# A fused attention and two-layer kernel: state rows times w_in in plain float32, one batch at a time

## The chip, the cores and the metric

The kernel runs on one core of one Trainium2 chip. The metric is the device time of one execution in microseconds (us); less is better. The shapes are fixed, and the program is fully unrolled: every instruction stands in one of the engines' instruction streams, in an order fixed when the program is built.

## What is computed

```python
scores = 0.125 * x @ state.T          # per batch b (8) and head h (8); x 512x64, state 32x64
a = softmax(scores); xread = a @ state
a2 = softmax(0.125 * state @ x.T); sread = a2 @ x
x = concat([xread, sread], rows)      # 544 rows per batch, 8 heads side by side: 4352 x 512
h = x @ w_in;  g = s * relu(h)**2 + b;  x = g @ w_out        # 512 -> 2048 -> 512
h = x @ w_in2; g = h * sigmoid(h);      out = g @ w_out2     # 512 -> 2048 -> 512
```

## The kernel before, in words

All the weights come in as 64-bit numbers and are made into 32-bit ones on the chip. `load64` fetches a pair of weight units (a unit is 128x512 numbers, 512 KB raw) into one of two `raw` buffers, `absw` (L189, ScalarE, "A" below) takes the absolute value of the high words, and `bits` (four VectorE steps at L197, L201, L206 and L211, "B") shifts and joins the words. The first layer has 16 units of w_in (i0 to i15) and 16 of w_out (o0 to o15).

A matmul here runs on TensorE in the rounded 32-bit type `float32r`, in one pass. To keep the accuracy, an operand is split into a rounded part and a rest (`hi_w` on ScalarE, `lo_w` on VectorE by way of `rest`, L232), and each product takes three matmuls: high times high, high times low, low times high. A matmul on operands of type plain float32 needs no split.

The first layer's input x is `a @ state` for the 512 rows of a batch, so the kernel doesn't form it. It forms G = state @ w_in for each batch and head (32 rows per head), and then `a @ G` for the batch: `mm1_a` (L566, "M1") multiplies G with the transposed softmax weights `at_h`, `at_l`. G is made once for all batches, at the start: `produce(u, p, at)` (L275) takes the unit u of w_in and the pair p of batches, and does three `float32r` matmuls 128x128x512 (L281) with the split state `sgh`, `sgl`. There are 16 units and 4 pairs, so 192 matmuls. Its result is copied out of PSUM (L229): for pairs 1 to 3 whole (`xr`, 128x512), for pair 0 in halves of 64 rows, one per batch (`pull_g`). `keep_g` writes it to `gd` in DRAM; `load_g` later fetches what a batch needs, and `split_g` splits it. Batch 0 is taken straight on (`first_g`).

The program has these stages on TensorE: the first block (batch 0: G for all batches, the softmax of batches 0 and 1, the conversion and split of all 32 units, and batch 0 through the first layer), then seven blocks for batches 1 to 7 and one for the state rows ("s"), each 16 x (M1 of 6 matmuls, `mm2` of 12 matmuls, L628, "M2"), then the second layer (`first_product` and `Chunks`, L902).

The order of the first block is written out by hand in the table `FIRST`, which `first()` reads name by name: L load of a weight pair, A and B its conversion, H and O (with i or o) the split of a unit, Sh and Sl the split of the state, P a `produce`, E the copy out of PSUM, D the write to `gd`, F the split of batch 0's G, M1, R (relu), S (square), T (times s, plus b), U (split), M2, and names with p or q the steps of the softmax of a half (four heads) of a batch. A star puts a step on VectorE that otherwise runs on ScalarE. Each engine takes its steps in the order of the table. PSUM has eight banks of 128x512: four (`ps_o`) accumulate M2's result, two (`ps_h`) take M1's, two (`ps_a`) are for the rest. In the later blocks `run` sets the order, with M2 three steps behind M1, and `extra` hangs the loads, the splits and the next batch's softmax between them.

A tile has the name of its place in SBUF (`v3`, `wh5`, `xr1`); the trace leaves the numbers out. `bank` is a tile in PSUM.

Of the kernel before, what the change touches and what calls it, by code (L numbers as in the profile page):

```python
# [22 lines left out]
P = 128  # L23
# [23 lines left out]
A.4 Lsbd.1 B.3.1 B.3.2 E.3.2 R.0 D.3.2 B.4.0 E.4.1 P.5.3.o B.3.3 R.1 D.4.1 M1.2 S.0 E.4.3 B.4.1
B.4.2 M1.3 S.1 D.4.3 Ho.1* Lxn.0.0 T.0 L.5 P.4.2.o R.2 F.2.0 p1mm.a E.4.2 Eb.5 B.4.3 Hi.6* E.5.1
D.4.2 Oi.6 P.5.2.o U.0.0 D.5.1 P.6.0.a Hi.7* p1rd Ho.0* Oo.1 T.1 P.6.2.h S.2 P.6.3.o E.5.3 D.5.3
p1nb p0sr.o Eb.6 U.1.0 D.5.0 Oo.0 U.0.1 Oi.7 Ea.6 p1ex P.6.1.o p1tr L.6 p0pu A.5 U.1.1  # L50
P.7.0.a E.5.2* D.5.2 R.3 P.7.1.a E.6.1 T.2* B.5.0 P.7.3.h E.6.3 D.6.3 S.3 M2.0 D.6.0 Ea.7 D.6.1
T.3 U.2.0 B.5.1 B.5.2 B.5.3 L.7 p1n0 F.3.0 M2.1 Eb.7 U.3.0 F.2.1 Hi.8 F.3.1 A.6 Oi.8 U.2.1
E.6.2 P.8.0.a M1.4 B.6.0 E.7.3 D.7.3 E.7.1 p1mx B.6.1 D.6.2 D.7.1 D.7.0 Lxn.1.0 Eb.8 U.3.1 R.4
Ho.2 B.6.2 M1.5 M1.6 D.8.0 Oo.2 p1n1 Ea.8 R.5 S.5 P.7.2.a P.8.1.h p1n2* R.6 B.6.3 A.7 P.8.3.a
p1sb L.8 M2.2 B.7.0 B.7.1 Ho.3 Hi.9 E.8.3 D.8.3 E.7.2 Oi.9 D.7.2 B.7.2 Oo.3 S.4 P.9.1.h
P.9.0.a S.6 T.4 U.4.0* p1en p1tu.a B.7.3 M2.3 E.8.1 D.8.1 p1s0 Eb.9 Ea.9 p1pl U.4.1 Ho.4
Hi.10* A.8 L.9 D.9.0 Oo.4 P.8.2.a P.9.3.h Oi.10 T.6 p1sr.a B.8.0 E.8.2 p1s1 E.9.1 B.8.1 E.9.3
p1s2 p1pu D.9.3 F.4.0 D.9.1 B.8.2 B.8.3 D.8.2 Lxt.1.1 P.10.0.h T.5 Ea.10 U.5.0 F.4.1 p1s3 L.10
Ho.5 Hi.11 Oo.5 A.9 p1s4 P.10.3.a M1.7 Oi.11 Eb.10 P.10.1.a M2.4 R.7 B.9.0 B.9.1 P.11.0.h
U.5.1 U.6.0 E.10.3 P.9.2.h Ea.11 Eb.11 D.10.3 q1mm.a E.10.1 D.10.1 S.7 B.9.2 B.9.3 E.9.2  # L60
P.11.1.h M2.5 Lsbd.2 F.5.0 q1rd Hi.12 L.11 U.6.1 Lg.0.0 Ho.6 F.5.1 A.10 Oi.12 E.11.1
B.10.0 B.10.1 M1.8 M1.9 q1nb D.9.2 D.11.1 D.10.0 B.10.2 p1ah T.7 R.8 U.7.0 Lxn.1.1 P.12.1.a R.9
B.10.3 q1tr P.11.3.h q1ex P.10.2.h q1n0 Oo.6 P.12.0.a S.8 E.11.3 M2.6 Ho.7 Hi.13* Oi.13
D.11.0 L.12 A.11 Ea.12 U.7.1 E.12.1 T.8* Oo.7 E.10.2 D.10.2 M1.10 B.11.0 B.11.1 S.9
Gh.0.0 U.8.0 D.11.3 Eb.12 D.12.1 M1.11 T.9 q1n1 q1n2* B.11.2 M2.7 B.11.3 U.9.0 R.10 U.8.1 L.13
Hi.14 q1tu.a A.12 Ho.8* Oo.8 P.11.2.a q1pl q1mx P.13.0.h R.11 P.12.3.a B.12.0 E.11.2 D.11.2
q1sr.a U.9.1 B.12.1 S.10 E.12.3 Eb.13 D.13.0 P.13.1.a q1pu Ea.13 D.12.0 D.12.3 Oi.14
P.14.0.h B.12.2 B.12.3 Hi.15* P.13.3.a S.11 E.13.1 D.13.1 Ea.14 P.12.2.h Ho.9 M2.8 Gl.0.0
E.12.2 Oi.15 D.12.2 A.13 q1sb q1en L.14 Oo.9 B.13.0 Eb.14 P.14.1.a E.13.3 P.15.0.h E.14.1 F.6.0*
q1s0 P.13.2.h B.13.1 B.13.2 B.13.3 Ea.15 D.14.1 P.15.1.a Eb.15 D.15.0 q1s1 P.14.2.a  # L70
# [17 lines left out]
def fused_kernel(ctx: ExitStack, tc, xt, xn, sbd, sg, w1, w2, sv, bv, out):  # L88
# [22 lines left out]
    turn = [0]  # L111

    def bank(at, shape):

        if at == "o":
            at = f"o{turn[0] % NC}"
            turn[0] += 1
        pool = {"h": ps_h, "a": ps_a}.get(at, ps_o)
        return pool.tile(list(shape), F32, tag=at, name="bank")

    def space(tag, shape=(P, S), dtype=F32R):
        return wpool.tile(list(shape), dtype, tag=tag, name=tag)

# [7 lines left out]
    xr = [space(f"xr{c}", dtype=F32) for c in range(NC)]  # L131
# [11 lines left out]
    again = [False]  # L143

    def tags(w):
        t, i = w
        if t == "o":
            return f"wh{i}", f"wl{i}"
        i = AGAIN[i] if again[0] else NU - RING + i % RING
        return f"v{2 * i}", f"v{2 * i + 1}"  # L150

    def load64(pair):
        t = rot("raw", 2, (P, 2, S, 2), U32)
        raw[pair] = t.rearrange("p i n t -> p (i n) t")
        for i, (k, u) in enumerate(pair):
            src = w1 if k in "io" else w2
            nc.sync.dma_start(
                out=t[:, i],
                in_=src[u + NU * (k in "oO")].bitcast(U32).rearrange("p (n t) -> p n t", t=2),
            )  # L160

    def new32(pair):
        t = rot("wf", 2, (P, 2 * S))
        w32[pair] = t
        for i, w in enumerate(pair):
            w32[w] = t[:, i * S:(i + 1) * S]

    def load32(pair):
        for t, u in pair:
            w32[t, u] = space(f"mid{u % 4}", dtype=F32)  # L170

            fg, c = divmod(u, NC)
            for q in range(4):
                r = q % 2 * D + c % 2 * NS
                nc.sync.dma_start(
                    out=w32[t, u][q * NS:(q + 1) * NS],
                    in_=kept[t, NC * fg + c // 2 * 2 + q // 2][r:r + NS],
                )
# [4 lines left out]
    def absw(pair, i=None):  # L183
        if not i:
            new32(pair)
        hi, tf = raw[pair][:, :, 1], w32[pair]
# [4 lines left out]
    def bits(pair, op, i=None):  # L191
        lo, hi, tf = raw[pair][:, :, 0], raw[pair][:, :, 1], w32[pair]
# [23 lines left out]
    def reorder(pair, i):  # L216

        x = w32[pair[i]]
        w32[pair[i]] = to = space(f"v{24 + i}", dtype=F32)
# [13 lines left out]

    def hi_w(w, dve=False):
        wh[w] = space(tags(w)[0])
        copy(wh[w], w32[w], dve)

    def lo_w(w):
        wl[w] = space(tags(w)[1])
        rest(wl[w], w32[w], wh[w])  # L240

    def split(hi, lo, x):
# [7 lines left out]
    sg_t, sgh, sgl = {}, {}, {}  # L250
    gd = {
        (p, fg): dram.tile([NC * P, S], F32, name=f"gd{p}_{fg}")
        for p in range(B // 2) for fg in range(4)
    }
    G = {}

    def load_sg(p):
        sg_t[p] = space(f"v{12 + p}", dtype=F32)
        nc.sync.dma_start(out=sg_t[p], in_=sg[p])

    def hi_sg(p, dve):
        sgh[p] = space(f"wh{12 + p}")
        copy(sgh[p], sg_t[p], dve)

    def lo_sg(p):
        sgl[p] = space(f"wl{12 + p}")
        rest(sgl[p], sg_t[p], sgh[p])

    def new_g(b, fg):
        i = 4 * ((4 * b + fg) % 3)  # L270
        G[b, fg] = [[space(f"v{i + 2 * j + k}") for k in range(2)] for j in range(2)]

    gp = {}
# [1281 lines left out]
```

## Time and profile before

| | |
|---|---|
| median of 3 runs | 1329.31 us (1329.28 to 1331.46) |
| span of the profiled execution, first to last instruction | 1328.2 us |
| the profiled execution's own time | only its span is given; it lies 1.1 us under the median of the runs |
| TensorE matmul busy | 1304.2 us (98%), 6928 instructions |
| VectorE busy | 993.5 us (75%) |
| ScalarE busy | 739.7 us (56%) |
| mean granted TensorE clock | 0.999 of full |

The trace holds one execution, with the start and the length of every instruction. An engine's busy time is a union over its instructions. Matmuls overlap: the next starts while the results of the one before still drain, so their cost is the distance between starts, not the recorded length. On VectorE, too, an instruction that doesn't depend on the one before starts a little before that one's record ends. "Idle before" is the time in which an engine had nothing running, and the releaser is what it waited for.

### The profile page before, as it was taken

What the parts mean: (1) busy time and instruction counts of PE and PEld (TensorE: products, weight loads), DVE (VectorE), ACT (ScalarE), POOL (GpSimd) and SP (SyncE); (2) the same over time, 40 slices, a digit from 0 to 9 for tenths busy, and PEclk for the clock granted to TensorE, in tenths of its full rate; (3) what the DMA queues carried; (4) which work ended last, traced back from release to release, by engine and by line L of the source; (5) the groups of instructions that cost most, each with busy time, mean ns of one, the idle gap of its engine ahead of it and who ended that gap; (6) DMA issues with size and microseconds to landing.
All of it is one profiled execution on the core that took longest, in us unless ns stands there. A gap on an engine that the chain in (4) does not pass through costs nothing.

```text
span 1328.2 us, 20865 instructions
## 1 busy us (share of the span) xinstructions
PE 1304.2 (98%) x6928; PEld 1131.3 (85%) x6928; DVE 993.5 (75%) x1794; ACT 739.7 (56%) x1360; POOL 0.7 (0%) x7
## 2 busy tenths in 40 slices
PE   5999999999999999999999999999999999999997
PEld 3678787878787878888988888999998888999997
DVE  8999797979797979865966757576777765565654
ACT  7999564555454545544665646465666634353541
POOL 0000000000000000000000000000000000000000
PEclk9999999999999999999999999999999999999999
DMA  8988556464655545434568475657699796777583
GB/s 305 306 302 281 208 191 198 157 223 143 212 174 201 177 158 167 161 107 134 179 198 293 175 259 190 240 181 242 222 320 357 264 278 186 198 221 230 170 258 86
DMA packets 182925, 284.01 MB, mean 214 GB/s; under 512 B 25632, under 2 KB 99360, under 8 KB 182816
## 3 DMA queue, kind: packets, MB, share of 16 engines
q1 hardware_dynamic: 182016, 282.28, 64.4%
q8 instruction: 54, 0.88, 0.3%
q10 hardware_dynamic: 800, 0.39, 0.1%
q14 instruction: 55, 0.45, 0.1%
HBM read 166.72 MB, written 115.87 MB: 213 GB/s over the span
## 4 chain that ended last, share of the span: by engine, by line
PE 92%; ACT 2%; DMA 2%; DVE 2%; issue 1%; SPq 0%; ACTq 0%
PE bank L902 49%; PE o L628 27%; PE ph L566 14%; DMA raw<-w 2%; PE bank L281 1%; ACT xr L229 1%; ACT wf L189 0%; PE bank L390 0%; PE bank L377 0%; DMA gd<-xr 0%; PE bank L503 0%; DVE wf L211 0%; DVE v L232 0%; DVE wf L197 0%; DVE wl L232 0%
## 5 line engine op out<-in xcount | busy, mean ns | idle before, releaser
L566 PE MATMUL ph<-xh,v 128*128 128x512 f32 (+1 forms) x640 | 205.2, 372 | 0.1
L628 PE MATMUL o<-gh,wh 128*128 128x512 f32 (+1 forms) x448 | 169.5, 378 | 0.0
L628 PE MATMUL o<-gh,wl 128*128 128x512 f32 (+1 forms) x448 | 169.3, 378 | 0.0
L628 PE MATMUL o<-gl,wh 128*128 128x512 f32 (+1 forms) x448 | 169.3, 378 | 0.0
L566 PEld LDWEIGHTS ph<-xh,v 128*128 128x128 f32 x640 | 117.2, 188 | 26.5 <-issue 5.0
L608 DVE SCALAR_TENSOR_TENSOR r<-r,s_sb 128x512 f32<-128x512 f32 (+1 forms) x128 | 91.4, 714 | 42.6 <-ACT r L607 42.3
L566 PE MATMUL ph<-xl,v 128*128 128x512 f32 (+1 forms) x320 | 117.8, 368 | 0.0
L607 ACT ACTIVATE r<-ph 128x512 f32<-128x512 f32 (+1 forms) x128 | 71.8, 561 | 81.6 <-PE ph L566 79.1
L613 ACT ACTIVATE gh<-r,b_sb 128x512 fp32r<-128x512 f32 (+1 forms) x96 | 66.5, 693 | 56.2 <-DVE r L608 55.9
L628 PEld LDWEIGHTS o<-gh,wl 128*128 128x128 f32 x448 | 84.3, 188 | 15.8
L628 PEld LDWEIGHTS o<-gl,wh 128*128 128x128 f32 x448 | 84.3, 188 | 15.5
L628 PEld LDWEIGHTS o<-gh,wh 128*128 128x128 f32 x448 | 84.3, 188 | 15.5
L902 PE MATMUL bank<-v,v 128*128 128x384 f32 (+1 forms) x304 | 91.6, 360 | 0.0
L902 PE MATMUL bank<-wh,v 128*128 128x384 f32 (+1 forms) x254 | 83.0, 355 | 0.0
L614 DVE SCALAR_TENSOR_TENSOR gl<-r,b_sb,gh 128x512 fp32r<-128x512 f32 (+1 forms) x96 | 68.5, 714 | 15.4 <-ACT gh L613 15.3
L628 PE MATMUL o<-v,wh 128*128 128x512 f32 (+1 forms) x256 | 75.1, 377 | 0.0
L566 PEld LDWEIGHTS ph<-xl,v 128*128 128x128 f32 x320 | 60.4, 189 | 9.5
L902 PE MATMUL bank<-wl,v 128*128 128x384 f32 (+1 forms) x183 | 61.4, 356 | 0.0
L902 PEld LDWEIGHTS bank<-v,v 128*128 128x128 f32 x304 | 56.4, 188 | 5.7
L628 PEld LDWEIGHTS o<-v,wh 128*128 128x128 f32 x256 | 46.9, 188 | 9.1 <-DVE o L641 0.5
L211 DVE SCALAR_TENSOR_TENSOR wf<-raw,wf 128x512 uint32<-128x512 uint32 (+1 forms) x65 | 52.9, 814 | 2.0
L206 DVE SCALAR_TENSOR_TENSOR wf<-raw,wf 128x512 uint32<-128x512 uint32 (+1 forms) x65 | 52.3, 804 | 0.2
(1059 smaller groups left out, 3163.2 us busy)
## 6 DMA issues: line engine op xcount, KB each, us to landing
raw<-w SPq DMA_DIRECT2D x80, 512.0 KB, 4.9
gd<-xr SPq DMA_DIRECT2D x48, 256.0 KB, 3.4
v<-gd SPq DMA_DIRECT2D x192, 64.0 KB, 2.2
go<-v SPq DMA_DIRECT2D x58, 192.0 KB, 2.2
go<-v SPq DMA_DIRECT2D x38, 256.0 KB, 2.3
v<-go SPq DMA_DIRECT2D x34, 256.0 KB, 4.4
v<-go SPq DMA_DIRECT2D x41, 192.0 KB, 3.6
wh<-go SPq DMA_DIRECT2D x39, 192.0 KB, 3.5
```

Of the source, the lines that this page charges most:

```text
L206: nc.vector.scalar_tensor_tensor(out=t, in0=lo, scalar=29, in1=t, op0=ALU.logical_shift_right, op1=ALU.bitwise_or,)
L211: nc.vector.scalar_tensor_tensor(out=t, in0=hi, scalar=0xC0000000, in1=t, op0=ALU.bitwise_and, op1=ALU.bitwise_or,)
L229: nc.scalar.activation(out=out, in_=x, func=AF.Copy)
L281: nc.tensor.matmul(t, a[p][:, cs], x[w], start=i == 0, stop=i == 2)
L566: nc.tensor.matmul(ph[:, :n], a, x, start=j == 0 and i == 0, stop=j == last and i == 2)
L607: nc.scalar.activation(out=r, in_=ph[:, :n], func=AF.Relu)
L608: nc.vector.scalar_tensor_tensor(out=r, in0=r, scalar=s_sb, in1=r, op0=ALU.mult, op1=ALU.mult)
L613: nc.scalar.activation(out=gh, in_=r, func=AF.Identity, bias=b_sb)
L614: nc.vector.scalar_tensor_tensor(out=gl, in0=r, scalar=b_sb, in1=gh.bitcast(F32), op0=ALU.add, op1=ALU.subtract)
L628: nc.tensor.matmul(po[c][:, :n], a, x, start=f == 0 and i == 0, stop=f == NF - 1 and i == 2)
L902: nc.tensor.matmul(bank[:, :n], a, x, start=start and j == 0 and i == 0, stop=stop and j == last and i == 2, skip_group_check=True,)
```

## The change

- **produce** works on one batch b and a group fg of four units, straight from the converted units `w32` and the unsplit state `sg_t`: eight matmuls in plain float32, each with 64 rows (one head) by 32 columns by 512, for four units and two heads each. They are laid so that the four units go to the four 32-row strips of the result, and the two heads to two banks: one tile 128x2x512 over two PSUM banks holds the whole G of this batch and group. There are 32 such steps (8 batches by 4 groups).
- The splits of w_in's 16 units and of the state (Hi, Oi, Sh, Sl) are gone from the first block.
- `pull_g` copies 128x1024 out of PSUM at once, `keep_g` writes 512 KB, `load_g` fetches 512 KB in one transfer. For batch 0, and for batch 1's group 0, `part_g` splits straight from PSUM into the places that M1 reads.
- The softmax of batch 0, and of batch 1, is done for both halves at once (`Both`), on tiles 128x1024. Batch 1's last steps (its sums' reciprocal, the scaling, eight transposes, the copy and the `read` of 32 matmuls) move from the first block into block 1.
- w_out's units 12 and 13 (`PLAIN`) are used unsplit in the first block: `mm2_plain` does four plain float32 matmuls 128x128x512 in place of twelve `float32r` ones. They are split at the start of block 1.
- PSUM: until the first M2 the four banks of `ps_o` are two tiles of two banks each (`o01`, `o23`) for produce and the softmax; `ps_a` is one tile of two banks.
- Tiles in SBUF are pairs (128x2x512); in the second layer `Place` hands out halves of them.
- The table FIRST is written anew; first come the loads of i0 to i3.

```diff
-FIRST_PAIRS = "i0 i1, i2 i3, i4 i5, o0 o1, i6 i7, i8 o2, i9 o3, i10 o4, ...
+FIRST_PAIRS = "i0 i1, i2 i3, i4 i5, i6 i7, o0 o1, i8 i9, o2 o3, i10 i11, ...
+PLAIN = (12, 13,)
...
-    ps_o = ctx.enter_context(tc.tile_pool(name="ps_o", bufs=1, space=bass.MemoryType.PSUM))
     ps_h = ctx.enter_context(tc.tile_pool(name="ps_h", bufs=2, space=bass.MemoryType.PSUM))
-    ps_a = ctx.enter_context(tc.tile_pool(name="ps_a", bufs=2, space=bass.MemoryType.PSUM))
+    ps_a = ctx.enter_context(tc.tile_pool(name="ps_a", bufs=1, space=bass.MemoryType.PSUM))
+    early = ExitStack()
+    ps_o = early.enter_context(tc.tile_pool(name="ps_p", bufs=1, space=bass.MemoryType.PSUM))
...
-    def produce(u, p, at):
-        c = u % 4
-        w = ("i", u)
-        t = gp[u, p] = bank(at, [P, S])
-        cs = slice(c * P, (c + 1) * P)
-        for i, (a, x) in enumerate(((sgh, wh), (sgh, wl), (sgl, wh))):
-            nc.tensor.matmul(t, a[p][:, cs], x[w], start=i == 0, stop=i == 2)
+    def produce(fg, b, at):
+        t = gp[fg, b] = bank(at)
+        p, s = divmod(b, 2)
+        rows = sg_t[p].rearrange("d (c s i n) -> d c s i n", c=NC, s=2, i=2)
+        for c in range(NC):
+            x = w32["i", NC * fg + c]
+            for i in range(2):
+                q = slice(i * D, (i + 1) * D)
+                nc.tensor.matmul(
+                    t[c * NS:(c + 1) * NS, i, :], rows[q, c, (s + c) % 2, i], x[q],
+                    start=True, stop=True,
+                )
+
+    def pull_g(fg, b, dve):
+        ge[fg, b] = t = rotated("xr", "xr0 xr1 q13")
+        copy(flat(t), flat(gp[fg, b]), dve)
+
+    def keep_g(fg, b):
+        nc.sync.dma_start(out=gd[b, fg], in_=flat(ge[fg, b]))
+
+    def part_g(fg, b, part, dve=False):
+        if part == 0:
+            new_g(b, fg)
+        hi, lo = both_g[b, fg]
+        if part == 0:
+            copy(flat(hi), flat(gp[fg, b]), dve)
         else:
-            nc.sync.dma_start(out=gd[p, fg][cs], in_=xr[p])
+            rest(flat(lo), flat(gp[fg, b]), flat(hi))
...
+    def mm2_plain(f, r):
+        for c in range(NC):
+            nc.tensor.matmul(
+                po[c], w32["o", f][:, c * P:(c + 1) * P], r, start=f == 0, stop=False
+            )
...
             elif what == "T":
-                r = act[x][0]
+                r = to = act[x][0]
+                if x in PLAIN:
+                    to = act[x][1].bitcast(F32)
...
         if bi == 1:
             add_g(0, (1, 2), 1, 1)
+            for n, u in enumerate(PLAIN):
+                add(1 + n, 2, hi_w, ("o", u))
+                add(1 + n, 2, lo_w, ("o", u))
+            one = softmax[1]
+            add(0, 0, load_all, 1, xn)
+            add(0, 0, load_sbd, 2)
+            add(0, 0, load_all, 2, xt)
+            for f, when, name, *args in (
+                (0, 0, "n0"), (0, 0, "n1"), (0, 0, "n2", 0), (0, 0, "n2", 1), (0, 2, "tu", "a"),
+                (0, 2, "pl"), (1, 2, "sr", "a"), (1, 2, "pu"),
+            ):
+                add(f, when, getattr(one, name), *args)
             add(2, 0, load_all, 2, xn)
```

How the order changes, at three places. First TensorE at the start of the program (before, then now; `bank` is PSUM, `sbd` the state for the scores, `wh` and `wl` here the split of a w_in unit or a place lent to x, `v` the state's split, `q` in the change a converted unit or the unsplit state):

```order
L440 MATMUL bank<-wh_231,sbd 64x512
L440 MATMUL bank<-wl_233,sbd 64x512
L281 MATMUL bank<-v_255,wh_262 128x512
L281 MATMUL bank<-v_267,wh_262 128x512
L281 MATMUL bank<-v_255,wl_272 128x512
L281 MATMUL bank<-v_255,wh_276 128x512
```

```order
L349 MATMUL bank<-xt,sbd 32x512 x4
L349 MATMUL bank<-q_245,sbd 32x512 x4
L286 MATMUL bank<-q_250,q_252 32x512 x4
L286 MATMUL bank<-q_260,q_252 32x512 x4
L286 MATMUL bank<-q_250,q_274 32x512 x4
L286 MATMUL bank<-q_260,q_274 32x512 x4
```

Before, the first product needs one converted unit and a split; now each step of two rows needs the four units of `q_250` and `q_260`.

Second, VectorE before the first M1 (before, then now; `wf` and `q` are units in conversion, `mid` the softmax, `nm`, `mx` and `sum` its small parts):

```order
L211 SCALAR_TENSOR_TENSOR wf_248<-raw_224,wf_248 128x512
L232 TENSOR_TENSOR wl_265<-v_229,wh_259 128x512
L232 TENSOR_TENSOR v_267<-wf_248,v_255 128x512
L232 TENSOR_TENSOR wl_272<-v_235,wh_262 128x512
L450 TENSOR_REDUCE nm<-bank 128x1
L232 TENSOR_TENSOR wl_289<-v_237,wh_276 128x512
```

```order
L202 SCALAR_TENSOR_TENSOR q_260<-raw_239,q_260 128x512 x2
L207 SCALAR_TENSOR_TENSOR q_260<-raw_239,q_260 128x512 x2
L516 TENSOR_REDUCE nm_301<-bank 128x2
L527 STREAM_TRANSPOSE mid_304<-bank 128x1024
L521 TENSOR_SCALAR nm_301<-nm_301 128x2
L540 TENSOR_REDUCE mx_312<-mid_304 128x32
L193 TENSOR_SCALAR q_308<-q_308 128x1024
L197 TENSOR_SCALAR q_308<-q_308 128x1024
```

The splits (L232) of the state and of w_in have left the stretch, and four units are converted ahead of the first softmax step.

Third, TensorE where block 1 begins (before, then now; `xh`, `xl` are the softmax weights, L628 and L701 are M2):

```order
L628 MATMUL o_1824<-v_1668,wh_663 128x512
L628 MATMUL o_1824<-v_1669,wh_663 128x512
L628 MATMUL o_1824<-v_1668,wl_700 128x512
L566 MATMUL ph<-xh_1152,v_1722 128x512
L566 MATMUL ph<-xl_1471,v_1722 128x512
L566 MATMUL ph<-xh_1152,v_1723 128x512
```

```order
L713 MATMUL bank<-gh_1211,q_1101 128x512 x4
L286 MATMUL bank<-q_803,q_274 32x512 x4
L286 MATMUL bank<-q_902,q_274 32x512 x4
L713 MATMUL bank<-gh_1285,q_1101 128x512 x4
L634 MATMUL bank<-xh_1320,q_406 128x512
L634 MATMUL bank<-xl_1324,q_406 128x512
L634 MATMUL bank<-xh_1320,q_407 128x512
L634 MATMUL bank<-xh_1320,q_406 128x512
L634 MATMUL bank<-xl_1324,q_406 128x512
L634 MATMUL bank<-xh_1320,q_407 128x512
L577 MATMUL bank<-ident,mid_1067 128x128 x8
```

Now the two plain M2 (L713) and a last produce stand ahead of block 1, and batch 1's eight transposes (L577) behind its first M1; before, M1 followed straight on M1 there.

## Rows read from the trace of the kernel before

**Rows 1.** Busy time by stretch: length, then PE, PEld, DVE, ACT, POOL, PEclk, DMA share, GB/s
```profile
0.00:36.48 36.48, 22.75 (x111) 14.78 (x112) 29.89 (x57) 28.42 (x50) 0.73 (x7) 1.00 0.86 303
36.48:136.91 100.43, 97.08 (x507) 75.39 (x506) 95.52 (x148) 93.86 (x162) 0.00 (x0) 1.00 0.88 301
136.91:202.50 65.59, 65.59 (x362) 52.70 (x361) 57.85 (x108) 36.33 (x62) 0.00 (x0) 1.00 0.52 179
202.50:667.00 464.50, 464.50 (x2594) 386.98 (x2593) 383.13 (x705) 236.17 (x413) 0.00 (x0) 1.00 0.52 171
```

**Rows 2.** Timeline of PE, first block: start, length, what, count
```profile
8.25 1.09 PE L440 MATMUL bank<-wh,sbd 128*64 128x512 f32 x1 [8.25 <-DMA wh<-xt]
...
10.71 1.22 PE L281 MATMUL bank<-v,wh 128*128 128x512 f32 x2
11.73 0.63 PE L281 MATMUL bank<-v,wl 128*128 128x512 f32 x1
...
36.48 0.39 PE L566 MATMUL ph<-xh,v 128*128 128x512 f32 x1
...
136.91 0.39 PE L566 MATMUL ph<-xh,v 128*128 128x512 f32 x1
```

**Rows 3.** Chain that ended last, in order of time: start, length, what
```profile
66.16 7.38 DMA raw<-w
...
112.46 3.44 PE bank L281 x15
...
128.91 8.16 PE o L628 x36
```

**Rows 4.** Timeline of PE: plain float32 matmuls, with the rows next to them
```profile
16.71 1.08 PE L440 MATMUL bank<-xt,sbd 128*64 128x512 f32 x4
17.71 0.73 PE L281 MATMUL bank<-v,wh 128*128 128x512 f32 x2
...
142.12 0.39 PE L628 MATMUL o<-gh,wl 128*128 128x512 f32 x1
142.44 0.63 PE L377 MATMUL bank<-xt,sbd 64*32 64x512 f32 x4
...
143.46 0.50 PE L566 MATMUL ph<-xh,v 128*128 128x512 f32 x1
```

**Rows 5.** Timeline of PE: transposes of a half, and a batch's read
```profile
103.35 0.60 PE L503 MATMUL bank<-ident,mid 128*128 128x128 f32 x4
103.70 0.71 PE L281 MATMUL bank<-v,wh 128*128 128x512 f32 x2
...
189.68 0.39 PE L628 MATMUL o<-gh,wl 128*128 128x512 f32 x1
...
191.03 0.50 PE L566 MATMUL ph<-xh,v 128*128 128x512 f32 x1
```

**Rows 6.** Timeline of DVE: the first steps, and block 1's first
```profile
4.96 0.43 DVE L197 TENSOR_SCALAR wf<-wf 128x512 f32<-128x512 f32 x1 [4.96 <-ACT wf L189]
...
9.47 0.68 DVE L232 TENSOR_TENSOR wl<-v,wh 128x512 fp32r<-128x512 f32 x1
10.07 0.68 DVE L232 TENSOR_TENSOR v<-wf,v 128x512 fp32r<-128x512 f32 x1
...
139.74 0.75 DVE L608 SCALAR_TENSOR_TENSOR r<-r,s_sb 128x512 f32<-128x512 f32 x1
```

**Rows 7.** Groups by form, 0 to 145 us, DVE and ACT: busy, mean ns, idle before
```profile
L211 DVE SCALAR_TENSOR_TENSOR wf<-raw,wf 128x1024 uint32<-128x1024 uint32 x15 | 18.3, 1222 | 0.3
L206 DVE SCALAR_TENSOR_TENSOR wf<-raw,wf 128x1024 uint32<-128x1024 uint32 x15 | 18.3, 1219 | 0.2
L197 DVE TENSOR_SCALAR wf<-wf 128x1024 f32<-128x1024 f32 x15 | 10.3, 688 | 1.5 <-ACT wf L189 1.4
L201 DVE TENSOR_SCALAR wf<-wf 128x1024 uint32<-128x1024 uint32 x15 | 10.3, 688 | 0.2
...
L229 ACT ACTIVATE xr<-bank 128x512 f32<-128x512 f32 x46 | 26.1, 590 | 0.8 <-DMA gd<-xr 0.5 <-PE bank L281 0.2
```

More of the change, by code (lines that the diff above doesn't have):

```diff
@@ L181, in keep, with absw @@
         nc.sync.dma_start(out=kept[w], in_=w32[w])
[L183 to L186, printed above, removed]
+    def absw(of, i=None, then=False):
+        if not i and not then:
+            new32(of)
+        hi, tf = raw[of][:, :, 1], w32[of]
         if i is not None:
@@ L336, in split_g @@
             new_g(b, fg)
-        split(*G[b, fg][j], staged.pop((b, fg, j)))
-    xt_t, xn_t, sbd_t = {}, {}, {}
-    at_h, at_l = {}, {}
-    free = iter([f"w{t}{f}" for f in range(8, 12) for t in "hl"])
-    def room(b, j, name, n=0, shape=(P, S)):
-        if b == 0 and j == 1:
-            return space(next(free), shape, F32)
-        return rot(name, n, shape) if n else space(name, shape, F32)
+        split(*G[b, fg][j], staged[b, fg][:, j])
+    sbd_t = {}
+    at_h, at_l, at_two = {}, {}, {}
     def load_sbd(b):
@@ L380, in score, with read @@
                 )
-    def read(b, halves):
-        o = halves[0].so = bank("a", [P, 2, D])
+    def read(b, halves, at="a"):
+        o = halves[0].so = bank(at, [P, 2, D])
         x = two.pop((b, False))
@@ L570, in mm1_a @@
     def mm1_a(f, k):
[L571 removed]
+        ph = bank("h", [P, S])
         fg, fs = f // 4, slice(f % 4 * P, (f % 4 + 1) * P)
@@ L770, in sum_w @@
         )
-        two = [space(f"v{(26 if t == 'I' else 28) + n}", dtype=F32) for n in range(2)]
+        x = pair("q13" if t == "I" else "q14")
+        two = [x[:, n] for n in range(2)]
         (s1, s2), (s3, s4) = ((x[:, :2 * P], x[:, 2 * P:]) for x in two)
@@ L811, in high @@
         def high(self):
-            self.two = [Place(static=True) for _ in range(2)]
+            self.two = [Place() for _ in range(2)]
             copy(self.two[0].t, self.raw.t)
@@ L871, in high @@
         def high(self, p, c):
-            two = [Place(static=True) for _ in range(2)]
+            two = [Place() for _ in range(2)]
             self.places[p].extend(two)
@@ L1042, in mm @@
                       "h": ("h", "h") if self.k % 2 else ("o2", "o3")}[name]
-                self.banks[name] = [bank(x, [P, S]) for x in at]
+                if name == "a":
+                    two = bank(name)
+                    self.banks[name] = [two[:, m] for m in range(2)]
+                else:
+                    self.banks[name] = [bank(x, [P, S]) for x in at]
             _, hi, lo = weights["O", i, p]
@@ L1184, in split_next @@
             load32(stream[i + 2])
+    softmax = []
     def first():
-        halves = {n + str(b): Half(b, j) for b in range(2) for j, n in enumerate("pq")}
+        softmax.extend(Both(b) for b in range(2))
         act = {}
@@ L1205, in one @@
                 bits(first_pairs[x], *at[1:])
-            elif what in ("Hi", "Ho"):
-                hi_w((what[1], x), dve)
-            elif what in ("Oi", "Oo"):
-                lo_w((what[1], x))
+            elif what == "Ho":
+                hi_w(("o", x), dve)
+            elif what == "Oo":
+                lo_w(("o", x))
+            elif what == "W":
+                idle = bank(x)
+                for _ in range(at[1]):
+                    nc.tensor.matmul(idle[:, 0, :P], ident, ident, start=True, stop=True)
             elif what == "P":
@@ L1332, in give @@
         def give(*tags):
-            add(f, 2, spare.extend, tags)
+            for tag in tags:
+                add(f, 2, vacate, tag)
         splits = [(p, c) for p in RIGHT for c in range(2)]
```

597 lines of the change are left out of this document (329 added, 268 removed).

## The prediction

> **What bounds the kernel now.** I read the busy times by stretch first. From 136.9 us on, where block 1 starts, TensorE is busy for all of every stretch shown, while VectorE has 11% or more to spare [rows 1]. What follows the first block is bound by TensorE alone, and a microsecond there is won only by taking work off it. The first block is different: from its first M1 (36.48) to block 1 (136.91) TensorE is busy 97%, VectorE 95%, ScalarE 93% of 100.4 us, and the transfers 0.88 [rows 1, 2]. All four are nearly full, and whatever lightens only one gains nothing. Ahead of the first M1, TensorE has 13.7 us without work, and VectorE sets the pace: it starts at 4.96 and is busy 29.9 us of the first 36.5 [rows 1, 6]. So the question is when block 1 starts, and what is put into it.
>
> **Prices on TensorE.** Matmuls overlap, so I take starts. 36 of M2 take 8.16 us, 0.227 each; 15 of the old produce 3.44, 0.229 each [rows 3]. For the new produce there is a row of the same shape: the scores of a batch are eight plain float32 matmuls of 64 rows by 32 columns by 512, two heads by four strips. The M2 before starts at 142.12 and would end its turn at 142.35; the M1 behind starts at 143.46 [rows 4]. So the eight cost 1.11 us together, where eight in a row would cost about 7. Each counts twice in the trace (x4 and x4 at 142.44 are the first of two passes). Row strips and column strips of the array work side by side, and this is what the change rests on. For a plain matmul 128x128x512 no row exists. The nearest is a pair of plain ones with 64 columns each: 16.71 to 17.71, 1.00 us for 128 columns [rows 4]. Bounds are 0.45 (were it two passes of 0.227) and 1.0; I take 0.9, near that pair, since its price holds two changes of the array's layout. A half's four transposes cost 0.35, and a batch's read 189.91 to 191.03, 1.12 [rows 5].
>
> **TensorE's work from the first M1 to block 1.**
> - Before: 63 of the 192 produce matmuls come ahead of it, so 129 x 0.229 = 29.5; M1 and 14 of M2, (96 + 168) x 0.227 = 59.9; batch 1's two scores 2.0, eight transposes 0.7, three half reads 1.7. Sum 93.8 in 100.4 us: 93% dense.
> - Now: 12 of 32 steps come ahead, so 20 x 1.11 = 22.2; (96 + 144) x 0.227 = 54.5; eight plain M2 matmuls 7.2, which is 1.8 more than the 24 that they replace; batch 1's scores 1.1, batch 0's read 1.1. Sum 86.1, and at the same density 92.2 us.
>
> **When the first M1 can start.** It needs batch 0's softmax weights and group 0's G, and the last of these is a VectorE step. Now four units are converted first: two took 4.96 to 9.47 [rows 6], so four end at 14.0. Then, in the new order, two pairs at 0.69 + 0.69 + 1.22 + 1.22 = 3.82 each [rows 7], ten steps of 1024 columns (seven of the softmax, its last split, two splits of G), and 0.6 of small ones. A step of 512 costs 0.60, the distance of two independent splits [rows 6]; at 1024 columns, between 1.13 (0.53 more, the difference of a 512 and a 1024 step, 1.22 against 0.69) and the 1.22 of a whole record; I take 1.14. Sum 14.0 + 7.6 + 11.4 + 0.6 = 33.6, and 0.8 for a wait on a weight pair: **34.4**, 2 us sooner than before, since the splits of state and w_in are gone from this path, though twice the weights must have come. TensorE has its 12 steps behind it by then: seven of group 0 between 14 and 28, one at a time with ScalarE's copies, five from 28.
>
> **When block 1 starts.** TensorE: 34.4 + 92.2 = 126.6, against 136.9: 10.3 sooner. VectorE: 66 splits of 512 become 28, plus 7 of 1024: -22.8 + 8.0 = -14.8. The conversion of one pair more in single units adds 0.7 (4.51 against 3.82), wider softmax steps save 0.7, starred steps (a copy of 1024, three squares, a relu) add some 2.5, and steps moved to block 1 and small ones save some 2.3. So its first step of block 1 comes 14.6 earlier than 139.74 [rows 6], at 125.1. ScalarE loses 78 copies at 0.59 [rows 7] for 26 of double width (0.59 to 1.18, I take 1.06): -18, and some 20 splits: it is no bound any more. The transfers move nearly the same weights and G in fewer pieces. TensorE and VectorE come out within 2 us of each other; the later one counts.
>
> **What block 1 takes over.** Eight transposes and a read: 0.7 + 1.1 = 1.8 us on TensorE, which has no gap there, so all of it counts. On VectorE it adds two scalings, a turn of the read and two splits, on ScalarE a copy and two splits: some 3 us each, in a block where VectorE is busy 57.9 of 65.6 us [rows 1]. That room hides it, if the queue isn't already late: the transposes stand right behind block 1's first M1, and wait until VectorE has gone through everything of the first block. By the sums it has, by 1.5 us. If it hasn't, TensorE loses what VectorE is late. The transfers that moved (batch 1's xn, batch 2's scores and x) stand at the head of block 1 on SP's queue, where the transfers' share falls to 0.52 [rows 1]; they are needed a step or two later. From there the matmuls are the same, in number and shape, to the end. PSUM's single two-bank tile in place of two of one bank, and halves of tiles in the second layer, cost nothing as long as TensorE's cover lasts: it never waits in the stretches shown from 136.9 on [rows 1].
>
> **The sum.** -10.3 + 1.8 = -8.5 us: the span goes from 1328.2 to 1319.7. The span lies 1.1 under the median, so the time is 1329.3 - 8.5 = **1320.8 us**, 0.64% faster. A measurement here tells about 0.2% (2.7 us) from no change.
>
> **The rivals.**
> - *No gaps are left.* With ScalarE at ease, the 7% of gaps could go: block 1 at 34.4 + 86.1 = 120.5, less 14.6 in all: 1314.7. Against it: VectorE's 125.1 stands in the way, unless its own 6.5 us without work (4.96 to 136.91, less 29.89 + 95.52 busy [rows 1, 6]) shrink too.
> - *A late start on a slow TensorE.* The first produce matmuls start 0.51 us apart (10.71, 11.73 after two), twice the 0.229 of later [rows 2, 3], like the lower of the two clock levels (1.2 GHz) though the granted clock reads 1.00 [rows 1]. The Trainium skill (TensorE: Matmul & The Clock Gate, "Why this matters for your kernels") says that idle gaps between bursts of matmuls bring the clock down again. The trace doesn't show that for the short gaps of 15 to 36 us, where the granted clock stays at 1.00. Now steps and gaps alternate from 14 to 34 us. At half speed each of the five steps of group 1 ahead of M1 costs 0.9 more, with the copies in between up to 4 us: first M1 at 38, time 1324.8. Weights that come late (one pair took 7.38 us in the chain [rows 3]) would cost about as much.
> - *Block 1 pays.* VectorE is late at block 1's start by the 6.5 us that it idles now, and the transposes wait: 5 us lost, 1326.
> - *Slower: halves of tiles in the second layer.* `Place` now prefers a half of a tile whose other half is in use, and so may hand out one that was given back just before, where until now the oldest place went. A load or a split then waits for a reader that has just run, and TensorE for it, in each of the 280 steps of the last product. It decides from 8.5 / 280 = 0.03 us a step; 0.08 us each gives 22 us, 1343. Against it: in the code the splits run five steps ahead, and a step is six matmuls.
> - *The eight don't run side by side.* Then a step costs 7.2 in place of 1.11, and 20 of them add over 120 us: above 1440. The scores' row [rows 4] speaks against it: same rows, columns and banks.
>
> **How the numbers follow.** My forecast, with bounds (start of M1 33 to 36, plain matmul 0.45 to 1.0, density 91 to 97%) from 1317 to 1324: 0.60. No gaps: 0.12. Late start: 0.13. Block 1 pays: 0.07. Slower by the halves: 0.06. Not side by side: 0.02. The range takes in the first four: 1314 to 1326.5; what is outside is 0.08 and the tails of the others, some 0.2. Faster by over 0.2% means below 1326.6: 0.60 + 0.12 + 0.13 + half of the 0.07 is 0.88. Slower by over 0.2%: 0.08 less a little for small stalls, 0.06; within 0.2%: 0.06.
>
> **What would show it.** Right: produce steps some 1.1 us apart when alone, with x4 and x4 starting together; the first M1 near 34.4; block 1's first M1 near 126.6, and VectorE's first step of it before; TensorE full from there on; 1.8 us more in block 1. Wrong: steps of 2 us or more; a first M1 after 37; a gap ahead of the transposes in block 1; any wait of TensorE in the second layer; block 1 starting after 133.

## The result, and the profile after

The changed kernel takes 1345.05 us (median of four runs, 1342.58 to 1345.64) against 1329.39 for the kernel before beside it: ratio 1.0112, 95% interval 1.0098 to 1.0127. It is 1.1% slower; 1320.8 was forecast, and the range ended at 1326.5. The profiled execution of the changed kernel has a span of 1342.8 us, 14.6 over the 1328.2 before.

From block 1 on the matmuls are the same but for what block 1 takes over, so each can be laid beside its twin in the other trace. The table gives what every stretch won (-) or lost (+), and in brackets how the kernel stands to the one before at the stretch's end. The last column is the fifth experiment below.

| stretch | predicted | changed kernel | fifth run |
|---|---|---|---|
| first M1 starts at | 34.4 | 33.90 | 33.85 |
| up to block 1 | -10.3 | -10.6 | -10.8 |
| block 1 | +1.8 (-8.5) | +3.0 (-7.6) | +2.1 (-8.7) |
| blocks 2 to 7 | 0 (-8.5) | +0.2 (-7.4) | 0 (-8.7) |
| s block | 0 (-8.5) | +4.5 (-2.9) | -0.2 (-8.8) |
| first product of the second layer | 0 (-8.5) | +17.4 (+14.5) | 0 (-8.8) |
| last product | 0 (-8.5) | 0 (+14.5) | 0 (-8.8) |

So the first block did what was forecast, and 22 us were lost later, where the diff hardly seems to reach. The busy times by stretch of the changed kernel (length, then PE, PEld, DVE, ACT, POOL, PEclk, DMA share, GB/s; the twins are [rows 1]):

```profile
33.90:126.30 92.40, 89.19 (x664) 51.31 (x657) 85.10 (x117) 68.23 (x96) 0.00 (x0) 1.00 0.74 262
126.30:195.76 69.46, 68.88 (x438) 55.36 (x437) 57.57 (x107) 37.25 (x62) 0.00 (x0) 1.00 0.65 233
195.76:660.00 464.24, 461.61 (x2557) 383.59 (x2556) 382.59 (x704) 236.06 (x410) 0.00 (x0) 1.00 0.51 171
660.00:740.00 80.00, 80.00 (x369) 66.68 (x369) 54.35 (x87) 47.63 (x85) 0.00 (x0) 1.00 0.68 230
740.00:960.00 220.00, 208.75 (x1068) 191.58 (x1067) 134.53 (x252) 110.48 (x226) 0.00 (x0) 0.98 0.56 198
```

Before, TensorE was full in every stretch from 136.9 on. Now it lacks 11.2 us between 740 and 960, and 2.6 between 196 and 660. In the first block it is busy 89.19 of 92.40 us. There ScalarE's busy time fell from 93.86 to 68.23 and VectorE's from 95.52 to 85.10.

The first block's own rows, from the timeline of PE (start, length, what, count), answer to [rows 2, 4, 5]:

```profile
33.33 0.61 PE L286 MATMUL bank<-q,q 64*32 64x512 f32 x4
33.36 0.61 PE L286 MATMUL bank<-w,q 64*32 64x512 f32 x4
33.90 0.51 PE L634 MATMUL bank<-xh,w 128*128 128x512 f32 x1
...
117.50 1.09 PE L286 MATMUL bank<-q,q 64*32 64x512 f32 x16
118.52 3.70 PE L713 MATMUL bank<-gh,q 128*128 128x512 f32 x8
122.15 1.09 PE L286 MATMUL bank<-q,q 64*32 64x512 f32 x16
123.17 3.70 PE L713 MATMUL bank<-gh,q 128*128 128x512 f32 x8
126.30 0.80 PE L634 MATMUL bank<-xh,q 128*128 128x512 f32 x1
...
128.09 1.04 PE L577 MATMUL bank<-ident,mid 128*128 128x128 f32 x8
128.88 0.47 PE L634 MATMUL bank<-xh,q 128*128 128x512 f32 x1
...
133.18 0.43 PE L362 MATMUL bank<-xn,mid 128*32 128x64 f32 x16
...
134.22 0.50 PE L634 MATMUL bank<-xh,q 128*128 128x512 f32 x1
```

A produce step takes 118.52 - 117.50 = 1.02 us, its two halves of four start 0.03 apart (33.33, 33.36), and a plain M2 unit takes 122.15 - 118.52 = 3.63, 0.91 a matmul. In block 1 the eight transposes cost 0.79 and the read 1.04. VectorE's queue reached block 1 in time:

```profile
125.41 0.16 DVE L556 TENSOR_SCALAR sum<-sum 128x2 f32<-128x2 f32 x1
...
125.81 0.88 DVE L566 TENSOR_SCALAR mid<-mid,sum 128x512 f32<-128x512 f32 x2
```

Where TensorE waits is in its list of waits from 126 us on (released by whom: us in total, times, longest); the kernel before has none from its block 1 on:

```profile
PE bank L1005 <- ACT q L229: 5.5, 3, 3.3
PE bank L1005 <- DVE q L852: 3.9, 3, 2.4
PE bank L634 <- ACT r L680: 3.2, 3, 2.4
PE bank L1005 <- ACT w L229: 1.8, 2, 0.9
```

L1005 is the second layer's matmul, L229 a copy out of PSUM, L852 a sum or difference, L1038 the silu (h times its sigmoid), L959 a load of x and L1041 the write of a result to DRAM; L634 is M1 and L680 its relu. TensorE waits for banks that nobody has read. Why they haven't been read stands a step further back. This is one such place, in the timelines of SP's queue, ACT and PE:

```profile
775.73 0.43 SPq L959 DMA_DIRECT2D gh<-x  x1
776.21 0.90 SPq L959 DMA_DIRECT2D q<-x  x2
777.21 0.85 SPq L1041 DMA_DIRECT2D go<-q  x2
783.74 0.79 SPq L1041 DMA_DIRECT2D go<-w  x2
```

```profile
776.66 0.63 ACT L1038 ACTIVATE q<-q 128x512 f32<-128x512 f32 x1 [0.80 <-DVE q L852]
782.59 0.60 ACT L229 ACTIVATE q<-bank 128x512 f32<-128x512 f32 x1 [5.30 <-DMA go<-q]
783.09 0.62 ACT L1038 ACTIVATE w<-w 128x512 f32<-128x512 f32 x1
783.61 0.59 ACT L229 ACTIVATE q<-bank 128x512 f32<-128x512 f32 x1
788.91 0.60 ACT L1038 ACTIVATE q<-bank 128x512 f32<-128x512 f32 x1 [4.71 <-DMA go<-q]
```

```profile
780.42 0.84 PE L1005 MATMUL bank<-w,q 128*128 128x512 f32 x3
783.25 0.50 PE L1005 MATMUL bank<-xt,q 128*128 128x512 f32 x1 [1.98 <-ACT q L229]
783.58 0.39 PE L1005 MATMUL bank<-raw,q 128*128 128x512 f32 x1
783.81 0.46 PE L1005 MATMUL bank<-xt,q 128*128 128x512 f32 x1
784.07 0.63 PE L1005 MATMUL bank<-raw,q 128*128 128x512 f32 x1
784.49 0.63 PE L1005 MATMUL bank<-sbd,q 128*128 128x512 f32 x1
```

A result that is finished goes to DRAM (`go<-q`, issued at 777.21). ScalarE's next copy out of PSUM is to go into the place that this write still reads, so it starts only at 782.59, 5.4 us after the issue. The steps behind the copy in ScalarE's stream come after it (783.09, 783.61). TensorE runs out of free banks and stands still for 1.98 us. From 784.07 on its matmuls are 0.42 us apart for a while, where 0.227 is the rule.

The longest wait for a relu, in the s block, has the same form, one layer earlier (L729 copies a block's result out of PSUM, L739 writes it, L171 loads a weight unit):

```profile
617.10 0.60 ACT L729 ACTIVATE r<-bank 128x512 f32<-128x512 f32 x1 [0.83 <-PE bank L701]
...
628.75 0.38 ACT L680 ACTIVATE r<-bank 128x256 f32<-128x256 f32 x1 [4.10 <-DMA x<-r]
```

```profile
618.25 6.75 SPq L171 DMA_DIRECT2D mid<-kept_i  x8
...
626.03 0.90 SPq L739 DMA_DIRECT2D x<-r  x2
```

The result lies in an `r` tile from 617.7 on. Its write is issued only at 626.03, behind eight loads on SP's queue, and the relu that is to use this tile again starts at 628.75.

Counted in the program itself: 280 places are taken for results of the first product. In the kernel before, 1 of them had been given back at most one step earlier; in the changed kernel 27 had. A step is six matmuls, 1.0 to 1.4 us. I call such places young. The writes of results haven't become slower. From issue to landing (us, shortest, median, longest), between 664 and 1000 us, of the kernel before:

```profile
DMA to landing us min/median/max: 1.8/2.3/6.3
```

and of the changed kernel:

```profile
DMA to landing us min/median/max: 1.8/2.1/6.3
```

### The profile page after: what moved, and what is told of

It is laid out like the page before. It is cut to its first block, busy times and chain, and to the rows that moved or that the text cites. A ratio compares the mean times of both kernels' runs of the same rounds, so it can differ in the third digit from the quotient of the medians.

```text
span 1342.8 us, 20818 instructions
## 1 busy us (share of the span) xinstructions
PE 1303.1 (97%) x7256; PEld 1102.7 (82%) x7256; DVE 979.5 (73%) x1745; ACT 705.3 (53%) x1273; POOL 0.7 (0%) x7
## 5 line engine op out<-in xcount | busy, mean ns | idle before, releaser
L701 PE MATMUL bank<-gh,w 128*128 128x512 f32 (+1 forms) x880 | 278.6, 380 | 0.8 <-ACT q L229 0.8
L634 PE MATMUL bank<-xh,q 128*128 128x512 f32 (+1 forms) x624 | 202.8, 374 | 4.4 <-ACT r L680 3.2
L701 PEld LDWEIGHTS bank<-gh,w 128*128 128x128 f32 x880 | 163.8, 189 | 39.1 <-issue 5.9
L701 PE MATMUL bank<-gl,w 128*128 128x512 f32 (+1 forms) x440 | 166.7, 379 | 0.0
L634 PEld LDWEIGHTS bank<-xh,q 128*128 128x128 f32 x624 | 114.4, 189 | 35.9 <-issue 6.9
L680 ACT ACTIVATE r<-bank 128x512 f32<-128x512 f32 (+1 forms) x128 | 71.9, 562 | 91.0 <-PE bank L634 74.0
L634 PE MATMUL bank<-xl,q 128*128 128x512 f32 (+1 forms) x312 | 114.9, 368 | 0.0
L1005 PE MATMUL bank<-q,w 128*128 128x384 f32 (+1 forms) x315 | 92.8, 357 | 3.9 <-DVE q L852 3.9
L701 PEld LDWEIGHTS bank<-gl,w 128*128 128x128 f32 x440 | 83.4, 190 | 15.0
L1005 PE MATMUL bank<-w,w 128*128 128x384 f32 (+1 forms) x319 | 88.0, 355 | 0.0
L701 PE MATMUL bank<-q,w 128*128 128x512 f32 (+1 forms) x384 | 87.5, 377 | 0.0
L1005 PE MATMUL bank<-w,q 128*128 128x384 f32 (+1 forms) x309 | 86.3, 358 | 0.0
L1005 PE MATMUL bank<-q,q 128*128 128x384 f32 (+1 forms) x283 | 81.9, 357 | 3.3 <-ACT q L229 3.3
L701 PEld LDWEIGHTS bank<-q,w 128*128 128x128 f32 x384 | 69.0, 188 | 13.6 <-DVE op L727 0.5
L634 PEld LDWEIGHTS bank<-xl,q 128*128 128x128 f32 x312 | 59.1, 189 | 9.0 <-DVE mid L566 0.2
L1005 PEld LDWEIGHTS bank<-q,w 128*128 128x128 f32 x315 | 58.4, 189 | 9.5 <-DVE q L852 4.9
L229 ACT ACTIVATE q<-bank 128x384 f32<-128x384 f32 (+3 forms) x70 | 42.9, 613 | 39.5 <-PE bank L1005 20.6
L1005 PEld LDWEIGHTS bank<-w,w 128*128 128x128 f32 x319 | 58.6, 188 | 4.9
L1005 PEld LDWEIGHTS bank<-w,q 128*128 128x128 f32 x309 | 56.8, 188 | 5.2
```

The lines of the kernel that those rows point to most:

```text
L229: nc.scalar.activation(out=out, in_=x, func=AF.Copy)
L634: nc.tensor.matmul(ph[:, :n], a, x, start=j == 0 and i == 0, stop=j == last and i == 2)
L680: nc.scalar.activation(out=r, in_=ph[:, :n], func=AF.Relu)
L701: nc.tensor.matmul(po[c][:, :n], a, x, start=f == 0 and i == 0, stop=f == NF - 1 and i == 2)
L1005: nc.tensor.matmul(bank[:, :n], a, x, start=start and j == 0 and i == 0, stop=stop and j == last and i == 2, skip_group_check=True,)
```

## The experiments

Theory A says that the second layer loses by the age of the places that results take. A2 says that the s block loses by `pull_out`, the copy of a block's results out of PSUM. Before, the third result tile went out from an `o` tile and only the fourth from an `r` tile. The diff gives the third result tile of a block a buffer of its own only while `ring` is empty; but `ring` is filled by the first w_out unit that is split, so the condition never holds. The third and the fourth result tile both go out from `r` tiles, of which the relus have three. The rivals: B, halves of one tile that make waits for each other; C, SP's queue or its transfers being late by themselves; and D, loads and splits that wait for matmuls, as the prediction had it.

**First: `Place` takes the oldest.**

```diff
-k = of[0] if of and len(whole) <= 8 else min(of[:1] + whole[:1])
+k = of[0] if of and len(whole) <= 2 else min(of[:1] + whole[:1])
```

> The change with one number of Place altered: it prefers a half of an opened tile only while two or fewer untouched tiles are left, in place of eight, and otherwise takes the oldest free place. Of the 280 places that results of the first product of the second layer take, 2 in place of 27 were then given back at most one step before. Theory A (a result's place is handed out again while its write to DRAM still reads it, so the copy out of PSUM waits, and TensorE for the bank): the gaps of TensorE between 783 and 951 us go and the 17.4 us lost there come back, the 4.5 us lost in the s block stay: 1345.05 - 17.4 = 1327.6, within 1325 to 1330. Rival B (halves of one tile make waits for each other, however old the place): as many halves are used, so it stays above 1338. Rival C (SP's queue and its transfers are late by themselves): the same transfers in the same order, so 1345 as before.

Measured: 1328.02 us, ratio to before 0.9983 (0.9974 to 0.9992). Matmul by matmul the second layer loses nothing, and in the whole trace after 126 us one line of waits is left, by the `r` tiles:

```profile
PE bank L634 <- ACT r L680: 2.0, 2, 1.6
```

A holds. B and C fall for the second layer, since halves, transfers and their order on SP's queue are still there. The s block lost 1.7 us here in place of 4.5, though nothing was changed for it. But the profiled execution (1325.22) is the fastest of the ten, 2.8 under their median, so the trace shows less than a usual execution loses; where the others lose it isn't shown.

**Second: a tile of its own for the third result.**

```diff
-            o = lasting()[:, 1] if i == 2 and not ring else rot("r", 3)
+            o = pair("xr1")[:, 0] if i == 2 and k != "s" else rot("r", 3)
...
-                for tag in ("xt", "xn", "xr0", "xr1", "q12", "q13", "q14"):
+                for tag in ("xt", "xn", "xr0", "q12", "q13", "q14"):
...
-                for tag in ("mid0", "mid1"):
+                for tag in ("mid0", "mid1", "xr1"):
```

The last four lines hand `xr1` to the second layer a few steps later, since a result still lies in it.

> The change with one buffer altered: the third result tile of a block goes out from a half of xr1, which nothing else uses in these blocks, and not from one of the three r tiles that the relus write. Theory A2 (two of the three r tiles are held by writes to DRAM, so the relus of the s block wait for them and TensorE behind them): the gaps at 623.7 and 629.2 us and the half-rate stretch behind them go, 4.5 us, and the 0.6 of block 1's wait on a relu: 1345.05 - 5 = 1340, if the second layer loses the same; its places come in another order (36 of 280 result places are at most one step old, in place of 27), so it may lose up to 6 more. Rival (the writes are late because SP's queue is behind its loads of w_in, and whatever tile they read from is missed next): s block loses the same, 1345.

Measured: 1347.8 us, ratio 1.0139 (1.0120 to 1.0158), not the 1340 expected. Yet the s block lost 0.3 in place of 4.5, and the 0.9 of block 1 came back, with the loads on SP's queue where they were: this speaks for A2. What came back there was lost again in the second layer, whose places now come in another order: 24.7 us in place of 17.4. Its waits of TensorE from 600 us on:

```profile
PE bank L1005 <- ACT q L229: 9.2, 4, 4.0
PE bank L1005 <- ACT raw L229: 4.6, 1, 4.6
...
PE bank L634 <- ACT r L680: 0.2, 1, 0.2
```

**Third: both.**

> Both edits: places as in the first run, result tile as in the second. If both causes are right and there is no third, all that the change lost after block 2 comes back: 1345.05 - 17.4 - 5 = 1322.7, within 1320 to 1325, faster than the kernel before by 0.5%. If only the places count, 1327.6; if only the r tiles, 1340; if neither, 1345.

Measured: 1324.52 us, ratio 0.9958 (0.9946 to 0.9971): faster than both kernels, and within the range given. That is 3.5 us under the first run, with intervals that don't touch, so A2 holds. TensorE waits once more after 126 us, 0.9 us on a relu of the s block.

**Fourth: the fault alone, in the kernel before.** Only results are changed; they take the newest place.

```diff
-                self.tag = spare.popleft()
+                self.tag = spare.pop() if newest else spare.popleft()
...
-            x = self.h[name] = Place(F32)
+            x = self.h[name] = Place(F32, newest=True)
```

> The kernel before the change, with one edit: a result of the first product takes the place that was given back last, not the one that has been free longest. 204 of its 280 result places are then at most one step old, in place of 1. It has no tiles opened in halves for these results. Theory A (the age of the place decides, because a write still reads it): the old kernel, which had no gap there, gets gaps of TensorE behind ScalarE's and VectorE's waits for writes to go, and slows by 20 to 130 us: 1350 to 1460. Rival B (sharing a tile in halves decides): no change, 1329.

Measured: 1376.56 us, ratio 1.0355 (1.0339 to 1.0371). Up to the second layer the trace is that of the kernel before; then the first product loses 45.2 us, in the same way. ScalarE's waits, and one of them in its timeline:

```profile
ACT v L935 <- DMA go<-v: 23.9, 11, 4.1
ACT wh L935 <- DMA go<-wh: 16.7, 6, 4.2
...
714.38 0.60 ACT L229 ACTIVATE wl<-bank 128x512 f32<-128x512 f32 x1 [6.62 <-DMA go<-wl]
```

A again, and this time with no result in a shared half.

**Fifth: the fourth result tile too** (against the third run).

```diff
+        if i == 2 and k != "s":
+            outs[1] = pair("xr1")
-        if i < 2:
-            o = outs[0][:, i]
+        if i < 2 or k != "s":
+            o = outs[i // 2][:, i % 2]
         else:
-            o = pair("xr1")[:, 0] if i == 2 and k != "s" else rot("r", 3)
+            o = rot("r", 3)
```

> The third run (both edits) with one more: the fourth result tile of a block goes out from the other half of xr1 too, so that no r tile is held by a write to DRAM ahead of the s block. In the third run one wait on a relu was left (0.9 us at TensorE, and with the slow matmuls behind it the s block lost 1.03). Theory: that comes back, 1324.5 - 1.0 = 1323.5. Rival (what the s block loses has another cause, such as the loads of w_in ahead of it on SP's queue): 1324.5.

Measured: 1322.60 us, ratio 0.9948 (0.9934 to 0.9961). TensorE waits for nothing after 126 us, and the span, 1319.4, is what the prediction's sum gave (1319.7). This comes that close by luck: the profiled execution is the fastest of the five, 1.3 under their median. The step from the third run is too small for these medians to tell; that the last wait is gone is seen in the trace.

**Sixth: the two w_out units split again in the first block** (against the fifth run). In the order, `Ho`, `Oo` and `U` of units 12 and 13 stand where the plain ones had none, their M2 is the three-pass one, and block 1 no longer splits them.

```diff
...
-                if x in PLAIN:
-                    mm2_plain(x, act[x][1].bitcast(F32))
-                else:
-                    mm2_a(x, act[x][1:], S)
+                mm2_a(x, act[x][1:], S)
...
```

> The fifth run with the two w_out units, 12 and 13, split in the first block as before the change and multiplied in three passes. In the change a plain unit took 3.63 us on TensorE against 12 x 0.227 = 2.72, so the two cost 1.8; unsplit they save VectorE four steps of 0.6 in the first block, two of which block 1 does later. If TensorE sets the end of the first block: 1.8 faster than the fifth run, 1321.7. If VectorE does: up to 2.4 slower, 1326. If the two are in balance: within 1 us of it.

Measured: 1323.59 us, ratio 0.9947 (0.9935 to 0.9960), the same as the fifth as far as these runs tell; a difference of some 2 us isn't ruled out. It fits the balance case, and the trace shows what is balanced. TensorE comes to block 1 at 125.92, not earlier to speak of than in the fifth run (126.14). VectorE comes to it at 127.06 (125.41 in the changed kernel), and the transposes wait 0.65 us for its scaling. That is the prediction's rival "Block 1 pays" on a small scale: the plain units cost TensorE time and keep VectorE ahead of it.

**Seventh: which tiles must be old.** The change with the fifth run's result tiles (third and fourth, not the third alone as in the second run, which the expectation names), and with the first run's rule for results alone.

```diff
...
-            k = of[0] if of and len(whole) <= 8 else min(of[:1] + whole[:1])
+            k = of[0] if of and len(whole) <= (2 if old else 8) else min(of[:1] + whole[:1])
...
-            x = self.h[name] = Place(F32)
+            x = self.h[name] = Place(F32, old=True)
```

> The second run (own result tile) with Place changed for the results of the first product alone: these take the oldest free place, all other tiles choose as in the change. Of the 280 results none then takes a place given back at most one step before, but 32 conversions, 5 loads and 12 splits do. Theory A (results' copies out of PSUM are what waits, for writes to DRAM): the second layer loses nothing, 1324.5 as the third run, within 1323 to 1326. Rival D (the loads and splits that take young places wait for the matmuls that read them, which is how the prediction had it): the loss stays for the most part, 1335 to 1348.

Measured: 1322.12 us, ratio 0.9941 (0.9928 to 0.9953). The kernel differs from the fifth run only in that loads, conversions and splits may again take young places, and it is level with it: the second layer loses nothing, and TensorE waits for nothing after 126 us. So it is the results, and D falls: young places for the rest cost nothing here. Against the second run it is 25.7 us less, of which the second layer makes 24.7; the other edit is the fourth result tile.

**Eighth: is it the burst of loads?** The three longest waits for a write in the second layer (5.3 to 5.7 us) came right behind the eight loads of the next piece's x.

```diff
...
-            add(k, 24, load_inputs, k + 1)
+            for n in range(8):
+                add(k, 24 + n, load_inputs, k + 1, n)
```

> The change with its places and result tiles as they are, but the eight loads of the next piece's x, which SP issues in one step of the first product, spread over eight steps, one each. Young places stay: 42 of the 280 results take one that was given back at most one step before. In the trace of the change ScalarE or VectorE waited 5.3 to 5.8 us for a write to go right behind these loads (776 to 783, 850 to 856, 917 to 922 us), where a write lands in 2.0 us in the median. Theory E (a young place costs TensorE only where its write lands late behind the burst of loads): the long waits go, and some 10 of the 17.4 us come back: 1335, within 1330 to 1338. Rival F (a young place costs wherever it is, the burst is chance): with 42 of them in place of 27 it is no faster, 1345 to 1355.

Measured: 1344.50 us, ratio 1.0116 (1.0097 to 1.0134), as slow as the change; the first product loses 18.9 us. The 1335 of theory E did not come: spread loads don't help, and the longest wait for a write is 6.5 us even so. From issue to landing the writes take as long as before (1.8 at least, 2.3 in the median, 6.7 at most). As its places also came in another order, with more young ones, this doesn't rule out that the burst lengthens single waits.

## Why the prediction was wrong

Point by point, along its own steps:

- **Prices.** Produce step 1.11: measured 1.02. Plain matmul 0.9: 0.91. Both were read from the nearest rows before, and held.
- **First M1** at 34.4: 33.90. Over the seven profiled kernels with this first block it lay between 33.5 and 35.2.
- **Block 1** at 126.6: 126.30. The work of 86.1 us, counted at the prices of the kernel before, took 92.4: 93% dense, as assumed. VectorE came to it at 125.4 (125.1 forecast). In the other six kernels block 1 started between 125.7 and 129.5, so this agreement is partly luck of one execution; the gain there is 7 to 11 us.
- **What block 1 takes over**, 1.8: the transposes and the read cost 0.79 + 1.04 = 1.83, as forecast. Block 1 as a whole lost 2.1 wherever no wait falls in (second, third, fifth and seventh run). In the changed kernel 0.9 more was lost around a wait of 0.58 on a relu, by the `r` tiles.
- **"From there the matmuls are the same, in number and shape, to the end"** is true, and was taken for more than it says. The step that failed is the one behind it: "halves of tiles in the second layer, cost nothing as long as TensorE's cover lasts: it never waits in the stretches shown". That TensorE never waited [rows 1] was a property of the old order of places, not of the work. With young places it lost 17.4 us. The `r` tiles, a line of the diff that the prediction didn't price at all, lost some 5 in this execution (0.9 and 4.5), and 3.5 by the medians of the first and third run.
- **The slower rival** had the rule right (a place given back just before) and the time nearly (1343), but for the wrong reason. It put the wait on loads and splits in the last product, with matmuls as readers. There the trace lost nothing, and the seventh run shows that young places for them are harmless. The waits were on the results of the first product, whose reader is a write to DRAM. The argument against it, that splits run five steps ahead, is right for splits. A copy out of PSUM has no such lead, because TensorE needs the bank back a few steps later.
- **Its chance**, 0.06, had no other argument behind it. The 27 young places against 1 could have been counted in the program beforehand.
- The other rivals: ScalarE came at ease and gaps stayed; no wait stood ahead of the transposes; the eight run side by side. Of the late start, the cause came and the effect didn't: the granted clock is 0.83 between 20 and 30 us, where the kernel before has 1.00, and the first M1 wasn't late. In the first and fifth run the clock stays at 1.00 there, and the first M1 starts no sooner (34.06 and 33.85).

With both faults mended the change is worth 0.5 to 0.6% (fifth and seventh run), 7.3 to 7.8 us by the medians, where the sum of the prediction gave 8.5: the price of the first block was right, and the term that it put at nothing was not.

## What to carry to other kernels

When a change touches how buffers are handed out, count for each kind of user how many steps lie between giving a buffer back and taking it again, and set that against how long its last reader takes: a buffer whose last reader is a write to DRAM is not free when the write is issued, but, here, 2 to 6 us later, and the issue itself can stand behind loads on the same queue. Here young buffers were harmless where work ran ahead, and dear where an engine had to empty PSUM in time. "The bottleneck never waits" describes the old schedule; whatever reorders the buffers has to earn it again.

## What the runs showed of the hardware

A wait of TensorE cost more than its length here. In the changed kernel the gaps in the first product add up to 5.5 + 3.9 + 1.8 = 11.2 us, and 17.4 were lost; in the second run 17.4 and 24.7, in the eighth 11.6 and 18.9. Matmuls at half rate stand behind two of the changed kernel's gaps, at 783.25 and 856.18, and the granted clock (the number before the DMA share) falls in those stretches:

```profile
740.00:780.00 40.00, 40.00 (x179) 33.10 (x178) 23.46 (x37) 18.92 (x33) 0.00 (x0) 1.00 0.59 207
780.00:800.00 20.00, 17.19 (x68) 13.45 (x67) 8.35 (x14) 6.72 (x12) 0.00 (x0) 0.91 0.48 180
800.00:840.00 40.00, 40.00 (x203) 36.27 (x202) 29.10 (x54) 24.43 (x49) 0.00 (x0) 1.00 0.56 207
840.00:860.00 20.00, 16.70 (x89) 16.38 (x88) 6.89 (x13) 6.17 (x14) 0.00 (x0) 0.91 0.63 212
...
870.00:880.00 10.00, 7.60 (x43) 6.96 (x42) 5.52 (x12) 3.99 (x10) 0.00 (x0) 1.00 0.37 131
```

The 0.42 us between matmuls from 784.07 on belongs to the lower of the two levels (1.2 GHz), the 0.227 elsewhere to the upper (2.4 GHz); ahead of the fall TensorE had stood still for 1.98 us, and ahead of the one at 856.18 for 3.30. Not every such gap does it: behind a gap of 2.36 us at 873.77, in the last row above, the clock stays at 1.00. By its length alone a gap doesn't tell here whether the clock falls. The Trainium skill (TensorE: Matmul & The Clock Gate, "Why this matters for your kernels") says that idle gaps between bursts of matmuls take the engine back to half rate; this trace shows it behind the gaps of 1.98 and 3.30 us and not behind that of 2.36. The prediction used that rule for the first block, where it cost nothing that shows; it counted in the second layer. The slow matmuls make up some 3 of the 6.2 us that were lost beyond the gaps (about nine with 0.2 us too much behind the first gap, nine with 0.15 behind the second), an estimate from the distances of the starts. The rest was not taken apart.

The s block shows the same on PE, behind its wait for a relu; the granted clock between 630 and 634 us is 0.57:

```profile
629.19 0.39 PE L634 MATMUL bank<-xh,q 128*128 128x256 f32 x1 [2.42 <-ACT r L680]
...
630.97 0.41 PE L701 MATMUL bank<-gh,w 128*128 128x256 f32 x1
...
633.53 0.41 PE L634 MATMUL bank<-xh,q 128*128 128x256 f32 x1
```

The twelve matmuls of 256 columns between the last two rows take 2.56 us, 0.213 each; at the rate of the kernel before (0.12 each) they would take 1.4. In the eighth run a wait of 2.8 us in the same place left the clock at 1.00.
